# Two zeroed key buffers, a third engine for the key spreads of layer 0, and a new order, in a two-layer attention and token-mixing kernel

## The chip, the cores and the metric

The kernel runs on one core of a Trainium2 chip. The metric is the time of one execution on the device in microseconds (us), less is better. The engines of the core have short names here, those of the profile: PE is TensorE (matmuls; PEld its weight loads), DVE is VectorE, ACT is ScalarE, POOL is GpSimd, and SP is SyncE, which in this kernel issues all DMA transfers. Each engine works through a queue of its own in order; an instruction that must wait for another engine or a transfer waits on a semaphore at the head of its queue, and everything behind it waits too.

## The reference

`x` has 2048 tokens of 512 features, in bf16. Two equal layers follow one another; each is a part A and a part B, with one set of weights for both layers:

```python
x = x + A(layernorm(x), wqkv, wo)        # H = 32 heads of Dh = 16, window W = 256
x = x + B(layernorm(x), w1, b1, w2, b2)  # F = 1792
# A: scores = q k / 4 ; kept where 0 <= query - key < 256 ; softmax ; times v ; times wo
# B: u = gelu(h^T w1 + b1), which mixes tokens: (512 x 2048) (2048 x 1792); y = u w2 + b2, transposed back
```

## The kernel before

**Recorded operations and a written order.** The function does not issue instructions as it runs. Each step is recorded with `op(engine:kind, function, reads, writes, cost, ..., alts)` (`Graph.op`, L108): what it reads and writes, an estimated cost in ns, and in `alts` other engines that may do the same. `ORDER` (L15 to L43) is a compressed text, made beforehand by a planner that works with these costs; for each operation in turn it holds the operation's number and which of its alternatives is taken. `replay` (L176) decodes it, puts every operation at the end of the queue of its engine, and takes buffers from the pools (`Pool`, L56) as it goes; a buffer that is taken again makes its new writer wait for its old readers. `emit` (L197) then writes the queues, with one semaphore for each engine and 24 for transfers in turn. So a new ORDER can change the place of any instruction, the engine of those that have alternatives, and which buffers meet.

**Tiles.** Tokens go in four groups of 512, m = 0 to 3. `qkv(m)` (L528) makes queries, keys and values of a group: normalised tokens are transposed (`transpose`, L532: on PE for m = 0, by a DMA transpose of SP, L535, for the others), then multiplied by wqkv (`proj`, L553, for q and k, each in four parts o = 0 to 3 of 8 heads; `vproj`, L610, for v). All matmuls of projections, of wo, of u's parts and of y go through one helper line, L506. Results leave PSUM by a copy on DVE or ACT: queries `evq` (L564), values `evv` (L620, L622) into `vst`, from where SP spreads them to `vb` with four transfers (`vz`, L625).

**Keys.** Scores use the keys as weights in a block-diagonal form, `kbd[P, 3, 4, 8, 2, 64]` (L344): three buffers (the pool `p_kv`), one for each group in use. For each block of 64 keys two copies stand side by side, h = 0 and h = 1; in copy h only the partitions of the head with that parity hold keys, and the other 16 of each 32 partitions hold zeros. Group 0 writes both copies from PSUM, multiplied by the 0/1 columns `par` (`evka`, L574 on ACT or L575 on DVE). For the groups after it a copy `evk` (L586 on DVE, L588 on ACT) takes the keys to a staging buffer `stg`, and the key spread `kz` takes them from there to `kbd`, in one of two ways: `f_kz` (L590) is eight transfers of 16 KB on SP (L595), which write only the partitions that hold keys and so need zeros in the others already; `f_kz2` (L598) is two multiplications by `par` on POOL or DVE (L600), which write the zeros too. One line sets who may do it:

```python
if not layer and m < 3:
    ways = ways[:0:-1]
```

In layer 0, groups 1 and 2 write key buffers 1 and 2 for the first time and may use POOL or DVE only; group 3 takes buffer 0 again, whose zeros group 0 has written, and may use SP; so may all groups of layer 1.

**Attention.** `attention` (L653) goes over chunks of queries (`CHUNKS`, L331). A score `sc` (L679) multiplies keys and queries into two pairs of PSUM banks; two `exp` (L694, ACT) take them to bf16 probabilities `pt` (7 buffers), 128 x 1024 at a time as a rule; `mask` (L715, POOL) multiplies the edge blocks of the window by 0/1 words `ldm`; `pv` (L732) multiplies by the values, whose 17th column is ones (the memset `one`, L454) and gives the softmax's sums. DVE transposes the result (`od`, L752) and takes reciprocals (`rec`, L756); `prod` (L758, POOL or DVE) multiplies; `od2` (L763) transposes back. I count scores from 0 in the order of PE; layer 0 has 76 of them.

**The rest of a layer.** `wo_block` (L768) multiplies by wo (`fwo`) and adds to x (`res`, L774); a layer norm follows: statistics on DVE (`stat` L464, `agg` L466), `rstd` (L477) on POOL, normalising `xh` (L484) on DVE. u is summed over token groups as they come: `u_part` (L827) for the first tokens, with sums kept in `uT` (`evu`), and `u_last` (L846) for the last ones (`ful`, L853; `addu`, L864; gelu on ACT, L868). y (`y_block`, L886, kind `fy`, and `y_last` for the last tokens) multiplies by w2 and adds to x (`resy`, L894). w1 and w2 come from HBM in pieces of 128 KB on SP (`load_w1`, L783, L788; `load_w2`, L798, L800); each new piece waits until a buffer is free.

**Start.** Before the first layer, POOL writes the identity (`ident`: a memset L380, two selects L381 and L383) and the triangle for the masks (`tri`, L440 and L441); DVE makes `par`, `half` and `ldm` from them (L433 to L449) and warms PE with 42 matmuls. The first tokens' statistics, rstd and xh lead to the first keys (L574, L575), the first score and the first exponential, which starts at 9.23 us.

Of the kernel before, what the change touches and what calls it, by code (L numbers as in the profile page):

```python
# [14 lines left out]
ORDER = (  # L15
    'c-qZYJ&5Dl6~40X%xYimfEE<c1_ks$3o7(L4;)aTLJJCLK>;l&phATU2NZCjfD0ukpa&{ks1U)03KvsM;lhOjQ@C*9VgfE)xNzaZg$ox`xNyLQ3l}-^-'
    ';DQ%9mqm*W-MJ@-Jf&5^PTUig=m&x8#EXp8bY!nO0MoWh9R2vM_t$7>+eNTltlTbIJQ3qL12EE&*!#1FRrHR{$V`+Fha<*Oj8l@rpfWY<@rHtgZr|~gK'
    '>GZ*|u*d({`H+-*Ru$I5mFHahx4wJ(M<^t+x1172kzX9J-<IS(;`TvM8#W`cBnkFhyRoV8VDjhMOcwGf6@i{tULAvv-6L*7t>4BNl`W%dRJnj#HaVxcO'
    'qaSa6l)qabixrBc~$CzHu^!aeM8wOVCpLhES0nCW_#*=7vWZfDv2$Jsnhr|ERcfK@6w%wQOa836zT_zipG$yi!RnIcu~kI94m_aQR`pSV89{oIJ^e&GA'
    '9y6=af|HhRACumQ@C=84oTo2hWtT&rXYlr9FZ03VS^*BkAKShxjhGDfDR9Ti`s<mp>gS}kabzF|KRvO3Y`V7r>`qrzC$2!Lhw>uapn~Y}Yx>!KPFu$}~'  # L20
    'ih@)%QS0^k!Z!gXr2ucGz_|I`^Nf4L=yna$ghYuVw|!Ho@RdAgnT+Q}G0RvsV{^iCc}_Dev}<i!0PLpL?am3gdov!>H1i0y-E9lkG0yYcvMl#;y<YEj?'
    'i-q3JO9#kSl*0Q>rHfjAN9KT_q|@XJABh0K6E;rp5r+A?H$hD{1yzTrE^>>*Evmt6_YTDqO6r=lC;ZO{AMGh6(Cy>hCw4-HX7hf&=`#*iHP-Tt(Gae7b'
    '{v|GO8d5^73(6Q5Fk%AG1uzVAxkxRqA#n3AW-mo<OLn>$<f#iQ@zsp6e>LS}hC}1t65GqTp3Ml_jbw+cx5)$E^;WtEif$DfF1_GfYoW6uQ$9@7jhba$1'
    '_Ex(y58G+L<9P#`114?H0}u#JaFg2?f_B1tkkkffW8-5ZTDAxR>N49kdUyWNrv#C5}RP=c^J+<^id*OwP^zYk9woA*+TX}aBR!$1c1Oec%QqNrAS{F=V'
    'MzrXDbI0*6XmIlf~uUzksN5Zs6=)^Qa8j=e<)+?-1p;ek5jXG5*bQ&?~U?5-`vl+%I%9F%mQ5Yf&WUAvjt7?veWL48;SrA3X^=L&FAiV+-bPe&UAh{Sa'
    '<@<5J-_K)#t=u&|K@?OpKmj2_jRZl(^ZnE_UBW6vCa3`kVIWt6WS9mZC@+^Z;yCjIXn_DKk>?#r$}*16vg|GNX(Jrp@q8e^<>;*C;*{rQ`KKfaQKME13'
    'O=}m7@%32r2(mR=vWsF?RL8Wf5EU@AY8iv<^@63Qz}sQD1z`Uj4co*Q^l&tfmaAog2!_RAxvb9u_7x=(81Y!Ay22v<phRIr_(*=v?K$eP`j<^T9(POVH'
    'iB&I3|Lc5C7Ij>-E3euzQyM!}tG8M3_*mDHX*LWN{fqI{jC}SglqIK~U|PstT<BzDI+mth(K-^BP)t9=FEyfa)aR2ObOtAPDvV=t>5Cqcc$|but>YwFi'
    'd51S5uLwBCK;RxfHs5fo4qwOUO!1-Do>=?#*E9S)l*G>xoF)tb#Z10`02@};ri`o7h0dCx0Zjli^v(glPhPBbyERcnk5Wb^>s-&ufaWoZg{7R=`s6b;m'
    '^U-wmARQmnxbgHWVRDrz;EU+~;n@qRtUkr#=({&IdMK`QCj&*(GC%%u6rfs)z{IK4vHy{tH`m^#ESe8vSI4|C_%21K|EfDx_(z9(FMlehSDeZJ+pob(5'  # L30
    '2Dea(495WP3W%^y>-u&FoLQ|ph2465({)=spTYFFnM%I_wF9drwK#_StX0;FBFC|JmSHt43&FYd-as~R#dR#mqVHG^a$On~XIjOyfLA^btcNpEqiJjnh'
    'r<oW0f$XPmZ3n@G>$Q78OESuD3TR8Yiv@TP60lQ#u^$q#*W+&b=6Z5Jtt6oV6Pu0!-R}LA^U?qg~9>qclsURDh(($@9rA6KqI=<3TWCp$knxD+kiTRoI'
    '94KJFcKZ)OtnJK%{`8Bn*EPLImUu0}}9p0M3G}xP`3|64$XhSJnAyJ_F{d>SQvT&wwY!aA?eCvwJ8`rgN*1cAgUiP^T&QpCV+WgwZq=v|g?L(IMFL;bg'
    'LG3(#HJhN2iIl4VW?gcleKzrGcC1~JS{H%UR*NCUnMs3Z(0+l>#nAXG(gK{UcG0~LzK@N~Z~Os5EAlq{2oF$&x@%l15!c6;}}?}0MpQ55^w4}u12AlIo'
    'v+8oma4x0!Bnide|p`llJ1@WoId0t)Q6gb~xUaIf{ASx+hu7Q^|fyavNSQ5?C^v1@RiFm>;@k*8(8?@nl9syS4>9n>0V(Tk7N<h+q?_-QdkHhU^Ydk#c'
    '*1);JVE4EfKTLFeF@5NbdX^;`Vqt6eRszk<Q?@TjE%j)lPNNCRJVpXSwtJ6IS40^?%~st}YatErTC{?IN05J@9#oTzQ1KPQpzmlD7~IJ9@%j1%Q;xs$;'
    'A6*rA&SDsRVk``ez|{DKKB0#mCLAn=tD*OXyvD7G4|D~!yYG(O68-!2$xEwFZgxryT1N3hW*6S6-+92C>8&uuLXBi{2!LT+GBII-xQVb6@`v2mrkg?46'
    '7$U%3mJz>Wn@0S$3YXv~L$%A4eT}UZ3%$j=L2P08ojdAk5N}pNGDS#Y=~orP9k{!Iw^*^7^dzo1m0W>G-Zz`W&$%`cI&o-t6HyhW}|2De4)t=Yh}gr_S'
    'hqHs_ES>S^b1GK50^H+F-_7jjiDQuUc2T(YIKuf^g=4ll^nzEL`5=IUh{bmaHtojT<XeL}8t^9Ot!0f*ox&X+%xlrlQ@oijrnUVn*@ugg!|IyLE|e4Hs'
    ')Djk*R>HZw1LuU!<`}p<=v#X~$Ux1_d?%aoiUlm11;mb0FM|=&}=LFivUyQ?-7?fdX`Rch0AJHp+y9~=uk)9wsMf<GuN|$9=I=?<$&w(Br2h>XE1LNBS'  # L40
    'DW3(dD9IA_wNngH)bkp?)PWa^$==E9Gf>n8;V48s*W-)DsV6t6Gpi3$K%vW76m>!RGs{oPL;aUB_(GX^!8X+YM!imaeRiyzpnoRj=o#LhE6T;duloFHB'
    'EMr`{{hz3RoV'
)  # L43
# [262 lines left out]
def bass_interleave_layers__sliding_block__mixer_token_mlp__prompt_kernel(  # L306
# [28 lines left out]
    with es:  # L335
# [117 lines left out]

        f_one = lambda e: e.memset(vst[:, :, :, :, 16:17], 1.0)  # L454
# [73 lines left out]
        def qkv(m, before, split, layer):  # L528
            tx, tq, tk = Tile(p_xhT), Tile(p_qT), Tile(p_kv)
# [23 lines left out]
            def proj(o, which, a, b, wide):  # L553

                n, key = b - a, (filler(m == 0), which)
                ft = key[0]
# [12 lines left out]
                if m == 0:  # L569
# [18 lines left out]
                   alts=[("scalar", lambda e: e.copy(stg[:, ts.slot, 0:n], at()), act_cost(n))])  # L588

                def f_kz(e):  # L590
                    got = []
                    for h in range(2):
                        for r in range(4):
                            p = 32 * r + 16 * h
                            got.append(e.dma_start(kbd[p:p + 16, tk.slot, o, a // 64:b // 64, h, :],  # L595
                                                   stg[p:p + 16, ts.slot, 0:n].rearrange("p (s n) -> p s n", n=64)))
                    return got
# [376 lines left out]
```

## Time and profile before

| | |
|---|---|
| runs before, us | 443.46, 442.91, 442.94 (median 442.94) |
| the profiled execution's own time, us | 441.94 |
| its span in the profile, us | 440.2 |
| granted TensorE clock | 1.000 |
| key spreads (kz) in layer 0: POOL, DVE, SP | 6, 3, 3 |
| key spreads in layer 1: POOL, DVE, SP | 3, 5, 4 |
| last exponential of layer 0 ends, us | 154.05 |
| last matmul ends, us | 436.6 |

The profile is of one execution. A row of a group gives the line, the engine and the operation, the tiles (written <- read) with their shapes, the count, then after a bar the busy time in us and the mean ns of one, and after another bar the idle time of the engine just ahead of them with what ended it. A row of a timeline gives the start and the length in us of a run of like instructions, with the idle time before it in brackets. Where several instructions of one engine overlap in its pipeline, the durations add up to more than the time that passes. The row of busy tenths cuts the span into 40 equal slices of 11.0 us.

### The profile page before, as it was taken

What the parts mean: (1) busy time and instruction counts of PE and PEld (TensorE: products, weight loads), DVE (VectorE), ACT (ScalarE), POOL (GpSimd) and SP (SyncE); (2) the same over time, 40 slices, a digit from 0 to 9 for tenths busy, and PEclk for the clock granted to TensorE, in tenths of its full rate; (3) what the DMA queues carried; (4) which work ended last, traced back from release to release, by engine and by line L of the source; (5) the groups of instructions that cost most, each with busy time, mean ns of one, the idle gap of its engine ahead of it and who ended that gap; (6) DMA issues with size and microseconds to landing.
All of it is one profiled execution on the core that took longest, in us unless ns stands there. A gap on an engine that the chain in (4) does not pass through costs nothing.

```text
span 440.2 us, 13923 instructions
## 1 busy us (share of the span) xinstructions
PE 422.9 (96%) x5992; PEld 187.6 (43%) x5992; DVE 311.1 (71%) x570; ACT 318.5 (72%) x364; POOL 225.4 (51%) x344
## 2 busy tenths in 40 slices
PE   7998998999999999999999999999999999999996
PEld 6543333344333444444444444443443444434452
DVE  6999888887887678475768868899987746512223
ACT  5999999999999913618999999999999950420000
POOL 2687898778677610011574877877666631000000
PEclk9999999999999999999999999999999999999999
DMA  7752423203225365533351651140223346773513
GB/s 243 206 96 64 112 51 66 60 13 72 44 43 147 106 177 158 145 99 78 92 112 37 140 118 25 47 102 17 51 60 86 90 132 179 205 200 112 157 53 101
DMA packets 99885, 45.09 MB, mean 102 GB/s; under 512 B 30064, under 2 KB 99824, under 8 KB 99824
## 3 DMA queue, kind: packets, MB, share of 16 engines
q1 hardware_dynamic: 99824, 44.21, 39.2%
q8 instruction: 47, 0.77, 0.7%
q14 instruction: 14, 0.11, 0.1%
HBM read 33.56 MB, written 2.10 MB: 81 GB/s over the span
## 4 chain that ended last, share of the span: by engine, by line
PE 71%; ACT 19%; DVE 3%; POOL 3%; DMA 2%; issue 1%; SPq 0%; DVEq 0%
PE PS L506 49%; ACT pt L694 19%; PE PS L853 8%; PE PS L679 7%; PE PS L732 7%; POOL pt L715 3%; DMA w2b<-in_B_w_dram 2%; DVE stats L464 1%; DVE rl L752 1%; DMA x_sb<-in_A_x_dram 0%; DVE xh_sb L484 0%; DVE x_sb L774 0%; PE PS L542 0%; DVE vst L620 0%; DVE x_sb L894 0%
## 5 line engine op out<-in xcount | busy, mean ns | idle before, releaser
L694 ACT ACTIVATE pt<-PS 128x1024 bf16<-128x1024 f32 (+1 forms) x304 | 281.5, 1042 | 11.8 <-PE PS L679 9.6
L715 POOL TENSOR_TENSOR pt<-pt,ldm 128x256 int32<-128x256 int32 (+1 forms) x270 | 177.2, 682 | 78.9 <-ACT pt L694 78.4
L506 PE MATMUL PS<-uT,w2b 128*128 128x512 bf16 (+1 forms) x294 | 69.7, 370 | 1.1 <-DMA w2b<-in_B_w_dram 0.9
L506 PE MATMUL PS<-xhT,wqkv 128*128 128x512 bf16 (+1 forms) x288 | 67.1, 358 | 2.7 <-ACT pt L694 0.8
L506 PE MATMUL PS<-xh_sb,w1b 128*128 128x512 bf16 x280 | 69.0, 381 | 0.4 <-ACT pt L694 0.3
L679 PE MATMUL PS<-qT,kbd 32*128 32x256 bf16 (+4 forms) x1488 | 60.7, 252 | 5.5 <-ACT pt L694 3.7
L477 POOL TENSOR_TENSOR rstd<-agg,mhalf 128x2 f32<-128x2 f32 (+1 forms) x33 | 23.2, 703 | 58.8 <-DVE agg L466 55.9
L894 DVE SCALAR_TENSOR_TENSOR x_sb<-PS,b2col,x_sb 128x512 bf16<-128x512 f32 x31 | 22.9, 744 | 40.8 <-PE PS L506 40.6
L679 PEld LDWEIGHTS PS<-qT,kbd 32*128 32x128 bf16 x1488 | 21.7, 93 | 65.1 <-ACT pt L694 44.8
L752 DVE STREAM_TRANSPOSE rl<-PS 128x1024 f32<-128x1024 f32 x32 | 39.7, 1240 | 13.3 <-PE PS L732 12.8
L868 ACT ACTIVATE uT<-rl,b1col 128x512 bf16<-128x512 f32 x28 | 18.7, 714 | 39.9 <-DVE rl L864 39.9
L732 PE MATMUL PS<-pt,vb 64*17 64x320 bf16 (+4 forms) x2976 | 43.0, 252 | 2.1 <-DVE x_sb L774 0.6
L464 DVE BATCH_NORM_STATS2 stats<-x_sb 128x6 f32<-128x512 bf16 x64 | 43.0, 680 | 2.2 <-DMA x_sb<-in_A_x_dram 1.5
L506 PEld LDWEIGHTS PS<-uT,w2b 128*128 128x128 bf16 x294 | 26.7, 98 | 33.6 <-issue 3.1
L506 PE MATMUL PS<-uT,pt 128*128 128x512 bf16 x168 | 40.9, 380 | 0.0
L732 PEld LDWEIGHTS PS<-pt,vb 64*17 64x17 bf16 x2976 | 31.3, 85 | 17.2 <-POOL pt L715 5.6
L506 PEld LDWEIGHTS PS<-xh_sb,w1b 128*128 128x128 bf16 x280 | 23.9, 98 | 32.1 <-issue 5.7
L853 PE MATMUL PS<-xh_sb,w1b 128*128 128x512 bf16 x168 | 37.0, 380 | 0.0
L506 PEld LDWEIGHTS PS<-xhT,wqkv 128*128 128x128 bf16 x288 | 23.9, 97 | 30.2 <-issue 6.0
L484 DVE TENSOR_SCALAR xh_sb<-x_sb,agg,rstd 128x512 bf16<-128x512 bf16 x64 | 30.6, 498 | 7.6 <-POOL rstd L477 7.6
L506 PE MATMUL PS<-wqkv,xhT 128*128 128x512 bf16 x128 | 34.4, 381 | 0.2 <-ACT pt L694 0.2
L506 PE MATMUL PS<-wo_sb,oT 128*128 128x512 bf16 x128 | 32.5, 381 | 0.3 <-DVE oT L763 0.2
(58 smaller groups left out, 313.1 us busy)
## 6 DMA issues: line engine op xcount, KB each, us to landing
w1b<-in_B_w_dram SPq DMA_DIRECT2D x112, 128.0 KB, 2.7
w2b<-in_B_w_dram SPq DMA_DIRECT2D x70, 128.0 KB, 2.6
pt<-in_B_w_dram SPq DMA_DIRECT2D x42, 128.0 KB, 3.0
vb<-vst SPq DMA_DIRECT2D x64, 68.0 KB, 2.1
out_dram<-x_sb SPq DMA_DIRECT2D x15, 128.0 KB, 1.8
x_sb<-in_A_x_dram SPq DMA_DIRECT2D x3, 512.0 KB, 8.1
wqkv<-in_A_wqkv_dram SPq DMA_DIRECT2D x4, 256.0 KB, 4.2
kbd<-stg SPq DMA_DIRECT2D x56, 16.0 KB, 2.0
```

The lines of the kernel that those rows point to most:

```text
L464: op("vector:stat", lambda e: e.bn_stats(st[:, 0:6], x_sb[:, t, :]), reads=[f"x{t}"], writes=[("st", i)], cost=dve_cost(512))
L477: op("gpsimd:rstd", lambda e: e.tensor_tensor(rstd[:, t0:t1, 0], agg[:, t0:t1, 1], mhalf[:, 0:1].to_broadcast([P, t1 - t0]), op=ALU.pow), ...
L484: op("vector:xh", lambda e: e.tensor_scalar(xh_sb[:, t, :], x_sb[:, t, :], agg[:, t, 0:1], rstd[:, t, :], op0=ALU.subtract, op1=ALU.mult), ...
L506: return e.matmul(o, lhsT=w, rhs=x, start=start, stop=stop, skip_group_check=True)
L679: last = e.matmul(bank(tt[r // 2], r % 2)[:, base + c0 * 64:base + (c0 + n) * 64], lhsT=kbd[32 * r:32 * r + 32, tk.slot, o, jj].rearrange( ...
L694: op("scalar:exp", lambda e, ts=ts, tp=tp, i=i, cols=cols: e.activation(probs(tp)[:, i, 0:cols, :], pair(ts)[:, :, 0:cols].rearrange("p r ...
L715: return e.tensor_tensor(v, v, m, op=ALU.mult)
L732: last = e.matmul(bank(t, h)[32 * r:32 * r + 17, i + q0 * 64:i + (q0 + n) * 64], lhsT=vb[64 * h:64 * h + 64, tk.slot, jj, 4 * o + r, :], r ...
L752: op("vector:od", lambda e, t=tod, tr=tr: e.transpose(rl[:, tr.slot:tr.slot + 2].rearrange("p a b -> p (a b)"), pair(t)), reads=[(tod, i) ...
L853: last = e.matmul(bank(tu, tt), lhsT=v()[:, sc - b0, k0 + tt * P:k0 + (tt + 1) * P], rhs=xh_sb[:, sc, :], start=(sc == b0), stop=(sc == NT ...
L868: op("scalar:gelu", lambda e, ft=ft, tt=tt: e.activation(uT[:, ft, :], rl[:, tmps[tt].slot], ACTF.Gelu_apprx_tanh, bias=b1col[:, ft:ft + 1 ...
L894: op("vector:resy", lambda e: e.scalar_tensor_tensor(x_sb[:, t, :], bank(ft), b2col[:, t:t + 1], x_sb[:, t, :], op0=ALU.add, op1=ALU.add), ...
```

## The change

Two operations are added: POOL fills key buffers 1 and 2 with zeros, each as 2048 float32 words a partition (4096 bf16). Every key spread reads their result. In layer 0 SP becomes the last alternative for the key spreads of all groups, and an assertion holds that it is not used for buffer 0 by groups 1 and 2. ORDER is new as a whole, made with the two zeros and the new alternative.

```diff
--- before.py
+++ after.py
@@ -13,33 +13,32 @@
 
 
 ORDER = (
...
 )
 
 def begin_order(n):
@@ -453,6 +452,9 @@
 
         f_one = lambda e: e.memset(vst[:, :, :, :, 16:17], 1.0)
         op("gpsimd:one", f_one, reads=["mhalf"], writes=["one"], cost=200, alts=[("vector", f_one, 200)])
+        for k in (1, 2):
+            op("gpsimd:zero", lambda e, k=k: e.memset(kbd[:, k].rearrange("p a b c d -> p (a b c d)").bitcast(dt.float32), 0.0),
+               writes=["kz0"], cost=1900)
 
 
         op("vector", lambda e: e.memset(stats[:, :, :, 6:9], 0.0), writes=["eps0"])
@@ -589,6 +591,7 @@
 
                 def f_kz(e):
                     got = []
+                    assert layer or m > 2 or tk.slot
                     for h in range(2):
                         for r in range(4):
                             p = 32 * r + 16 * h
@@ -601,9 +604,9 @@
                                                0.0, op0=ALU.mult, op1=ALU.add)
                     return last
                 ways = [("sync", f_kz, 700), ("gpsimd", f_kz2, 1340), ("vector", f_kz2, 2 * dve_cost(n, 0.25, ptrs=1), True)]
-                if not layer and m < 3:
-                    ways = ways[:0:-1]
-                op(ways[0][0] + ":kz", ways[0][1], reads=[ts] + [("par", h) for h in range(2)],
+                if not layer:
+                    ways = ways[:0:-1] + ways[:1]
+                op(ways[0][0] + ":kz", ways[0][1], reads=[ts, "kz0"] + [("par", h) for h in range(2)],
                    writes=[(tk, "k", o, h, k) for h in range(2) for k in KEYS(a, b)], cost=ways[0][2], lock=len(ways[0]) > 3,
                    issue=5600.0, dma=ways[0][0] == "sync", parts=8, prio=-2e5, alts=ways[1:])
 
```

What the new order does, in counts and places. PE has the same 5992 matmuls. Key spreads in layer 0: POOL 5, DVE 2, SP 5 (both of group 1 for o = 2 and 3, one of group 2, two of group 3); in layer 1: POOL 5, DVE 4, SP 3. Products (`prod`): POOL 17, DVE 15 (12 and 20 before). Key copies (`evk`) on ACT 3 (4 before), first-group key multiplies (`evka`) on ACT 3 (4 before), query copies (`evq`) on ACT 8 (6 before), copies of u's parts (`evu`) on ACT 4 (3 before). The memset `one` goes from POOL to DVE.

On POOL the first zero stands behind the two selects of the identity and ahead of the first two rstd; the triangle's memset and select stand behind these. The second zero stands behind the mask of score 6. On SP, the spread of group 1's o = 2 follows two value spreads, and the spread of o = 3 follows six loads (w1, w2). On PE the order of scores is the same; the work ahead of each score in layer 0 differs by at most 1.7 us. The value matmuls of scores 16 to 20 come in two halves, which both stand between scores 23 and 24 before; in the new order the first half stands ahead of score 23 and the second between scores 23 and 24, and score 23 gets other PSUM banks. At the end, three groups of y's matmuls stand ahead of the last matmuls of `u_last`.

More of the change, by code (lines that the diff above doesn't have):

```diff
@@ L15 @@
 ORDER = (
[L16 to L39, printed above, removed]
@@ L40 @@
-    ')Djk*R>HZw1LuU!<`}p<=v#X~$Ux1_d?%aoiUlm11;mb0FM|=&}=LFivUyQ?-7?fdX`Rch0AJHp+y9~=uk)9wsMf<GuN|$9=I=?<$&w(Br2h>XE1LNBS'
-    'DW3(dD9IA_wNngH)bkp?)PWa^$==E9Gf>n8;V48s*W-)DsV6t6Gpi3$K%vW76m>!RGs{oPL;aUB_(GX^!8X+YM!imaeRiyzpnoRj=o#LhE6T;duloFHB'
-    'EMr`{{hz3RoV'
+    'c-pmAJ&5br6~40X?7Q#nO}GI)P@x3{?t&H+(1HS5&;t=vsL+BI^uUD+2VA&tp@0`uxKQE31QjkE@Pdm8DB!|{3l}aNaN)v*3l}b?aN)v*3l}B~!Nmk}W'
+    'Y2i)_hy&u%kCMCbfx=yzVn^$SnedODN2knQDjVp+hTzTLQLETf#aB><9Od%mi3M?<Bv@LI(W~R#HwZM-OBrR37wYfj;FKfJL}zKI<ekLOg9W^&=<wGB3'
@@ new lines @@
+    'R=#6~%)nwmRL-rY(OlolcVRY&xHdZ<Ch!jrmPC41BQ~iekCUzpNF4g3m0|v?rw^Hu#saOt_|LTvIvUP)eo!WHN!LEXxSPpQ@^amdmVOVhwR$y+16!*wJ'
+    '}uJ`XnAcxyYhedpBcb)=ii^?EHy(u6P2LQxL<FyK2r9HeQ#M|Znj4FF*LcZyP3EEn?yg-M}4&bAs1M&r>~QP^NeBq?~`Znr6IJ8`eqlbO`$-gen$6Pnc'
+    '|5%qY^8qHE>f38O5N_nxUR;$xc3aj-}R9?U)rA=|Sds7Vuwc1GKy;@kU(sEj<_`c_r$}q9+!6}16P|`F>EqIFW*wRLl?;!-{d~T-oH^gy9qmgK5ws!2l'
+    'F*b(dDVnZDk*4XoLSa)?(*gi4g9nDuVzH;2w`4pXTXwf=iK1@6rMFrwLI6VuyGXk<j$@J}2qj4ZXwYh9u-R-_zdxnqw|Kp}%WSjV-fcI5?fbhutQ^Oyc'
+    'zu7r_V)jBoVEA*-i_yz@hFb*axpOHi$UKs$78eG?GA<m*EM$zi_;!suIu)aq}go3UiG?EF2`}BRyUHwI2>BWzR@6XFs)vX%b8WHl_kcd5-yiVBUCCu_}'
@@ new lines @@
+    'w7z;i1W@YOFVFa8*-*xnPn61k{y*qI@Mu;{)9(NlV7fX1ha36i1HZ)M|b$3@a^Y`Z26li!v-dS!QqnyPcz{B104dGF)BFxDLh@rG-*LahggPuoJVqsn>'
+    'G~R{(Ne84W8C2u_GhB+(Wn(-b9HlDMS!@I7lv<Tb+>bCn+s=x``xR93u5RxI1L3Iyn`X^<N`NJSVfGcoO_SsHaZ9kh86(EZw{gb1h}^(Xy4LVY#jLsLM'
+    'VPNm)Mv}xu)WG_Z`Ba|dcb>>S5DJbjEXl5mv>I$b)wU-Tzuo5&-093_Oby6(3Zd*ery-jFrnz3m+u8SGwT=i5}byQ79Xyv$jWJ{`U@UbK@8TVvmIJE0b'
+    'Y}LdCQ$#0<Sgn@IAy}bMu;LN~IErXZR1m=IsweZl&62lIdcARPG*UR6ir?P0l;1;CzkmykoC?^eQrS_|YPYmnO^g0e`#x^Okny$zYyjP;h7%YMevtvBP'
+    'mz$pU{I|(z^a5yJis)H5~c52#YPwwi<L^D0K<ZyAZ6%K0%5Ui_=k)T33*KjB!!OAe!FjiDrovfTjP~s8mrX;lxs`@S<oEROK)#GwEdu%5aLFo0cs>!mL'
@@ new lines @@
+    'v@+>1&<N59kM#X!>8ZY(I?s@^{~9dW`W+?R!N5W!di5+v$|y#bPwsZnw5Qv?2fQR<QbfHlIu*ux<q5fqX?Sr2!p|+@WPNHk-{fL<P%&gDW6~-4>+?Qsp'
+    '(``+GnJ7H=!cLYe0p4VJVL)@SwJc-(BVM%e3BR5eK62Wspa<tQy?0jkG!4<pw{UX}s~o2KV@t|N*L^C*BKdAjMCmY&Jy+A^(~X&7HQt^*Q!a6Namx{H_'
+    'THvNb6cRu2rgGw2ex#D+sHC;C?$cn12iPS72I2kCErU4_g_ZoP;4Z~r!r~=vm$;0{lPxIMK*C(8}Rkbi24M!2E#Ar0cu<GDzV>U|*0gU5QKtYmao7e<*'
+    'JMH%Uy}fVkK#%*t=>QJh?znDJPhfT&!>cNa6)`9W1tX|bE8c3g^SmXH#4$ipTnkb!C?tv6<PSbBaM!h6jQ<S}&x1nbh>)+EWm}lIvl()yQ&-yU2(i}4g'
+    'hGWf4Fc7LsH<&Fqlk0g4}6@-kTtPnG=%c^aKJb87DLEZtJboGF_gjC4A#YHI2n&akj6n84u`{8x0^svT;xF23TqHRjEk75QKYIv-z%3rRw`p`V_%YLzU'
@@ new lines @@
+    '70EnPxq+EHzy<3<(kqN>#@G^B^k^4-bq|Xc)%Cw)gj0gjYyZJEa-$49eVm{LgWgi-TiE-a;)S{XXaEmrc}YpjMpt6+-H9^p~g}Mc646#)SevSSm7zNul'
+    '8TmUYLllIfk6m1u4wdDao%3RS2g1`;BUkbof3#7t~3N)cfU=!*2N-Qs-F<Hpoz)qufS_a@$SJN4xfE!y)%8P$N_jgS(I;zkonQ|Le|Mgg1va>_??P$&j'
+    'L2})5w0ZG^Mku6(_>xsB1mzr`z)%7-VbhRu=CO05g6{U}L9ceIG)D$RjzVF*M=TzD4#0R#S6AEcb(Po2}u(>)|t-!l+s^G!4w@l@O+>ujxBTvZPT?c*)'
+    '+;(7C8cLBiE)582rKm<h40gbYHB_|0pf1a48b^B%icGZ`6w77ecZ;K9r5F}V6&(4#*hD}xw+8-O85M)THZ@Qc%>b$8Sv5OC_km?_y?S+Oze1mAf*^d-t'
+    'n7BY;C6!^TUa<5Liy}d{=EL<*VDZG({;2{6XQJC@#Cv}{(7?<{AJhKKKrO~)x4aV%e{E?oAZ%B_9?pwr#JX<iBG2|xtwt96!68Ar#AQvo#&pXg@rd)8='
@@ L43 @@
+    'Tzw(7PW2_uLYWkEbx50e;-)3Ej+7Fai7(KJ*Om%blK&Yvu&uV_aS^e8CanrStuNBzhrQDEDLN<WBt`4F75Pa_EV3&+wi7xjM6Oo+h9RfS*U5L4929X`v'
+    'qr;WZJ?Uj_7w0QGb2H!psrKRZ5;EPElhZfMqVlgoYnLTqwZxa3Y8MOWg0o&xi^@cHBStC0N!`5>X*;QUcWP6CoYzT_`Q<R9N(LsR(aAmm?kJCDwe=RT5'
+    '{GZN&9sOVzs#eiJyH2dbli;L4_PUBP3VSL4#&xGUegqKKl9E(r6ik}_MU(!%Gf6c$_<po;#mmoO1{js1vX)}K8IzF!bzJx^hSxEpy$X$}*?2m9Ql2=mr'
+    'p$va&J-lG0@Vwx&JY37fvnoFqypw*P&viNRvFl1nejyqCU;P&@A}f3<UcbgcKMe1)YX34@{o0QH7qHM$z5'
 )
```

## The prediction

> **What bounds the kernel now.** Line numbers are those of the kernel before. I read first how busy each engine is, then the busy tenths in 40 slices, then the chain of work that ended last. From the page:
>
> ```profile
> PE 422.9 (96%) x5992; PEld 187.6 (43%) x5992; DVE 311.1 (71%) x570; ACT 318.5 (72%) x364; POOL 225.4 (51%) x344
> ...
> ACT  5999999999999913618999999999999950420000
> POOL 2687898778677610011574877877666631000000
> ...
> PE 71%; ACT 19%; DVE 3%; POOL 3%; DMA 2%; issue 1%; SPq 0%; DVEq 0%
> ```
>
> The matmuls fill 96% of the span on average, but the ACT row shows nines in slices 2 to 14, that is from 11 to 154 us, layer 0's attention: there the exponentials are back to back and TensorE has gaps. From about 154 us on TensorE is the bound: it is busy 10.00 of 10 us in each stretch from 160 to 290 us in the busy time by stretches, and after 356 us only transfers of w2 stop it. The chain agrees: ACT holds 19%, all of it in layer 0, and PE 71%. An edit in layer 0's attention is worth what it does to the exponentials; one in layer 1 what it does to TensorE.
>
> The timeline of ACT from 40 to 66 us, around the first key spreads (start, us, ..., idle before and releaser):
>
> ```profile
> 42.64 7.44 ACT L694 ACTIVATE pt<-PS 128x1024 bf16<-128x1024 f32 x8 [0.38 <-PE PS L679]
> 49.88 0.67 ACT L588 CAST stg<-PS 128x512 bf16<-128x512 f32 x1
> 50.35 2.05 ACT L694 ACTIVATE pt<-PS 128x1024 bf16<-128x1024 f32 x2
> 53.44 13.10 ACT L694 ACTIVATE pt<-PS 128x1024 bf16<-128x1024 f32 x14 [1.04 <-PE PS L732]
> ```
>
> ACT loses 1.04 us at 53.44, ahead of score 23's exponential, whose probability buffer the value matmuls (L732, right behind that score on TensorE) have to free; 0.38 at score 18; and 0.47 (50.35 less 49.88) to a copy of keys.
>
> **The two zeros.** Neither is in the trace, so I bound them by POOL's memsets:
>
> ```profile
> L380 POOL MEMSET ident<- 128x128 bf16 x1 | 0.2, 204 | 0.3 <-POOLq L959 0.3
> L454 POOL MEMSET vst<- 128x128 bf16 x1 | 0.7, 650 | 0.0
> L385 POOL MEMSET mhalf<- 128x1 f32 x1 | 0.1, 98 | 0.0
> ```
>
> 128 elements a partition take 204 ns, one takes 98: (204 - 98) / 127 = 0.83 ns an element. A zero is 2048 float32: 98 + 2047 x 0.83 = **1.8 us**. If time goes by bytes, float32 elements cost twice a bf16 one: 3.5 us. L454, 4.3 ns an element, writes one element in each 17 and is no model for a contiguous write (it would give 8.9 us). I take 1.8, the rows nearest in shape, and keep 3.5 as the upper end.
>
> The first zero stands on POOL behind the two selects that make the identity and ahead of the first two rstd. In POOL's timeline:
>
> ```profile
> 1.56 0.29 POOL L383 TENSOR_SCALAR_AFFINE_SELECT ident<-ident 128x128 bf16<-128x128 bf16 x1
> 1.81 0.29 POOL L441 TENSOR_SCALAR_AFFINE_SELECT tri<-tri 128x128 bf16<-128x128 bf16 x1
> 3.98 0.56 POOL L477 TENSOR_TENSOR rstd<-agg,mhalf 128x1 f32<-128x1 f32 x1 [1.88 <-DVE agg L466]
> ```
>
> POOL is free from 1.85 (select's end) to 3.98, that is 2.13 us; the triangle's two operations move behind the rstds, where only the masks wait for them, from 12 us on. At 1.8 us the zero ends at 3.65 and costs 0; the cover is DVE's statistics. At 3.5 it ends at 5.35, 1.4 us late, and rstd, xh, the first keys and the first exponential are one chain: +1.4 whole. The second stands behind score 6's mask at about 23 us, where POOL waits 1.11 us for the exponential of score 7; masks have several scores of slack, so 0 (at 3.5 us too). The Trainium skill (GPSIMD Engine Reference, "3.1 Elementwise — side-by-side cycle accounting") puts a tight loop on this engine at 1.8 cycles an element, 512 in 769 ns; by that a zero would take an estimated 3.1 us and the start would be about 1 us late. The rows above, at 0.83 ns, speak against it.
>
> **DVE from 10 to 40 us.** The busy time by stretches gives DVE 9.89, 9.77 and 9.53 of 10 us there, so what it is given extra is late. The new order gives it one key multiply pair that ACT had (L575, 0.87 us for two in its timeline), and puts a statistic (0.68 us) ahead of copies that a score waits for: **+1.55 us** by scores 13 to 17. The memset of ones that moves to it is a row of 0.17 us and fits in the 0.81 us that is left idle. Bounds: 0 (all of it in gaps) and +2.2 (with a second statistic). ACT works less by 0.2 to 0.9 us before these scores, which gains nothing while DVE is late.
>
> **Scores 18 to 23.** This lag eats stalls of before: score 18's 0.38 goes (the score is late anyway), and so does the key copy on ACT, 0.47. Of the 1.04, half goes: the first value block now stands ahead of score 23 and frees the buffer in time, but it has taken the PSUM banks that this score had, which now waits for the second exponential of score 22. From that exponential's end a score takes 0.40 us and its exponential starts 0.06 later, so some 0.5 stays: -0.5. The bounds: at score 72, where value matmuls stand ahead of a score that waits in the same way, ACT lost 0.90, which leaves -0.14; -1.04 if the matmuls are early. Late next are the masks of these value matmuls. Net with the lag: 1.55 - 0.38 - 0.47 - 0.5 = **+0.2 us** (from -1.9 to +1.2).
>
> **The key spreads moved to SP.** In layer 0, SP takes five instead of three, POOL five instead of six, DVE two instead of three; DVE and POOL win 0.7 to 1.45 us each, beside ACT's bound: 0. But each spread on SP is eight transfers, and SP issues in order:
>
> ```profile
> 92.24 6.15 SPq L595 DMA_DIRECT2D kbd<-stg  x8
> ...
> 106.04 5.64 SPq L595 DMA_DIRECT2D kbd<-stg  x8
> ```
> ```profile
> kbd<-stg SPq DMA_DIRECT2D x56, 16.0 KB, 2.0
> ```
>
> The first new one follows two value spreads (vb, which end at 49.8 in SP's timeline): 49.8 + 6.15 + 2.0 landing = 58.0. Score 26, its user, starts at 58.38 before. The second: transposes end near 59.3; + 5.8 + 2.0 = 67.1, used by score 31 at 67.5. Margins of 0.4 us each: I take **0**. Behind them on SP wait w1 transfers and transposes of the third group, needed after 70 us: 0. Bounds: -0.5 (POOL, 9.6 of 10 busy from 50 to 70 us, gives masks earlier) and +1.6 a spread, from the slowest landing of this tile (3.6 us against 2.0).
>
> **The rest.** Layer 0 after score 31 has the same order on TensorE to within 1.7 us of work: 0. Layer 1 gives POOL two spreads (1.45 each) and two products (L758, 1.06 against 0.79 on DVE) more; TensorE bounds and a score of slack hides each: 0 to +0.5, taken as 0. The tail:
>
> ```profile
> 388.81 1.47 PE L506 MATMUL PS<-uT,w2b 128*128 128x512 bf16 x6 [0.52 <-DMA w2b<-in_B_w_dram]
> ...
> 395.35 1.90 PE L506 MATMUL PS<-uT,w2b 128*128 128x512 bf16 x8 [0.42 <-DMA w2b<-in_B_w_dram]
> ```
>
> TensorE loses 0.94 us to w2. The new order mixes the first output matmuls, whose w2 came early, with the last matmuls of u, so the late w2 blocks are met later: -0.6 (from -0.94 to +0.9, the same wait twice).
>
> **Sum.** 0 (zeros) + 0.2 (start to score 23) + 0 (spreads) + 0 (the rest) - 0.6 (tail) = -0.4 us. The profiled execution took 441.94 us (span 440.2, 1.7 around it): 441.5. The median of the runs shown is 442.94, 1.00 above: **442.5**. A measurement of this kernel tells about 0.2%, 0.9 us, from no change; the forecast lies inside.
>
> **Rivals.**
> 1. *Forecast*, 442.5, own range 441.6 to 443.3: 0.42, of it 0.15 below 442.05.
> 2. *A key spread on SP lands late* (other side). Place: scores 26 and 31; it decides from 0.4 us of delay on. If one lands like the slowest, 3.6 us, ACT stands 1.2 us; with SP held by a transfer ahead of it as long again, 2.0: 443.7 to 444.5; both: up to 446.5. For it: a margin of 0.4, and eight transfers in line. Against it: the median of 56 landings is 2.0. 0.17, all slower.
> 3. *The lag is not recovered*: DVE stays full and the stalls of scores 18 and 23 only move: +1.55 instead of +0.2, 443.9. For it: DVE is 9.12 of 10 busy from 50 to 60 us too. Against it: 7.84 from 60 to 70. 0.13: 0.03 within, 0.10 slower.
> 4. *A zero is long or stands in DVE's way*: 1.4 us at the start, 443.9. The listing of the normalising line shows how far POOL can hold DVE (ns, least, median, most):
>
> ```profile
> L484 DVE TENSOR_SCALAR xh_sb<-x_sb,agg,rstd x64: 314/407/1118, 4.7 to 369.8; 128x512 bf16<-128x512 bf16 x64
> ```
>
>    314 ns at 79.38 with POOL idle, 1118 at 283.30 where POOL's product had begun at 283.21. An xh that starts within the second zero would wait up to 1.8 - 0.4 = 1.4 us, on a DVE that is full: the same 443.9. The Trainium skill (SBUF — State Buffer, "Who interferes with whom") has the rule: a DVE operation in a two-port mode and a POOL operation exclude each other for a whole instruction. By that rule the trace agrees (0.31 to 1.12 us). Against the case: near 23 us DVE mostly reads PSUM. 0.08, slower.
> 5. *More gain*: the lag stays in DVE's gaps and the tail wins all: -1.38 - 0.94 = -2.3, 440.6, or half of it, 441.7. 0.17, faster.
> 6. *The change does not do what it says*: one POOL spread and one DVE spread fewer free nothing that bounds, and the rest is a reshuffle that evens out: 442.9. 0.03, within.
>
> Faster 0.15 + 0.17 = 0.32; within 0.27 + 0.03 + 0.03 = 0.33; slower 0.17 + 0.10 + 0.08 = 0.35. The range, 440.4 to 444.8, takes in case 5 and case 2 with one late spread.
>
> **What would show it.** Two POOL memsets of 1.8 us, the first ended before 3.98; the first exponential near 9.23. The exponential of score 17 late by 1.0 to 1.6, that of score 24 within 0.3 of 55.27. An idle of ACT of some 0.5 before score 23, none over 0.3 before 26 and 31. The last exponential of layer 0 ends near 154.2 instead of 154.05. TensorE's idle for w2 near 0.3. The forecast is wrong if the first exponential is late, if ACT idles on kbd transfers, or if layer 1 has gaps that it had not.

## The result and the profile after

The changed kernel took **441.01 us** (median of 5 runs, 440.41 to 441.39) against 442.94 (5 runs, 441.96 to 443.53): a ratio of 0.9957, 95% interval 0.9941 to 0.9972, or 1.9 us less. Measured once more later, beside other runs of the kernel before, it gave 0.9955 (0.9941 to 0.9968). That is faster by more than the 0.2% that I had set as the bound; I had forecast 442.5, inside that bound, with 0.32 for faster. The time lies in the whole range, but below the forecast's own range of 441.6 to 443.3, and three quarters of the gain were not in my sum.

The profiled executions differ by less than the medians: 441.33 us after (span 439.6) against 441.94 (span 440.2). The reason is that the shown profile of before is one of its faster executions; a second profile of it took 443.92 us. One pair of profiles is not enough for an effect of this size, and most of what follows rests on seeing the same place in many.

The page after, the lines that answer to those shown of before:

```profile
PE 423.1 (96%) x5992; PEld 187.3 (43%) x5992; DVE 306.8 (70%) x562; ACT 317.8 (72%) x364; POOL 234.2 (53%) x352
...
ACT  5999999999899921628799899999999960530000
POOL 4799779878876521011576577879876541000000
...
PE 77%; ACT 18%; DVE 4%; issue 1%; POOL 0%
```

TensorE has the same work; POOL has 8.8 us more, the two zeros, products and layer 1's spreads; in the chain, DMA's 2% are gone, and those were mostly transfers of w2 at the end. POOL's timeline at the start and near 23 us:

```profile
1.66 1.80 POOL L456 MEMSET kbd<- 128x2048 f32 x1
4.00 0.56 POOL L479 TENSOR_TENSOR rstd<-agg,mhalf 128x1 f32<-128x1 f32 x1 [0.54 <-DVE agg L468]
...
22.91 1.80 POOL L456 MEMSET kbd<- 128x2048 f32 x1
```

Each zero takes 1.80 us. The first ends at 3.46, and rstd, at 4.00 (3.98 before), still waits 0.54 us for DVE's aggregate, not for the zero. ACT's timeline, the stretches that a wait opens:

```profile
22.43 29.88 ACT L697 ACTIVATE pt<-PS 128x1024 bf16<-128x1024 f32 x32 [0.49 <-PE PS L682]
52.91 9.27 ACT L697 ACTIVATE pt<-PS 128x1024 bf16<-128x1024 f32 x10 [0.60 <-PE PS L682]
62.92 10.19 ACT L697 ACTIVATE pt<-PS 128x1024 bf16<-128x1024 f32 x11 [0.74 <-PE PS L682]
```

At 22.43 (score 7) DVE's lag shows. In the chain ahead of it stands a normalising multiplication (xh) beside POOL's masks, more than twice as long as the like one in the kernel before (first line before, second after):

```profile
19.83 0.37 DVE L484 TENSOR_SCALAR xh_sb<-x_sb,agg,rstd 128x512 bf16<-128x512 bf16 x1
19.60 0.94 DVE L486 TENSOR_SCALAR xh_sb<-x_sb,agg,rstd 128x512 bf16<-128x512 bf16 x1
```

At 52.91 (score 23) 0.60 is left of the 1.04 us of before; the wait at 62.92 (score 28) was 0.05 before. TensorE's timeline shows no engine or transfer of the kernel that it waited for there, but a gap inside the score itself, five matmuls in; score 58 has another:

```profile
61.67 0.36 PE L682 MATMUL PS<-qT,kbd 32*128 32x128 bf16 x5
62.53 0.34 PE L682 MATMUL PS<-qT,kbd 32*128 32x320 bf16 x7 [0.50 <-issue]
...
120.05 0.39 PE L682 MATMUL PS<-qT,kbd 32*128 32x128 bf16 x9 [0.49 <-issue]
```

How the time of the two first profiles parts, from the starts of the exponentials and the end of the matmuls (us, after less before; all work on TensorE is the same, and where its order differs between two points the work is taken out):

| up to | after less before |
|---|---|
| first exponential | +0.01 |
| score 8 | +0.82 |
| score 17 | +0.85 |
| score 24 | -0.53 |
| score 30 (gap inside score 28) | +0.15 |
| score 75, end of layer 0's attention (gap inside score 58) | +0.76 |
| score 151, end of layer 1's attention | +1.16 |
| last matmul | -0.55 |

So the whole gain of this pair, 1.71 us, is made behind score 151. There TensorE's timeline of after has no wait. That of before has the two waits for w2 that were shown with the prediction; first the lines just ahead of them, then those of after:

```profile
386.41 1.89 PE L506 MATMUL PS<-uT,w2b 128*128 128x512 bf16 x8
...
391.41 3.51 PE L506 MATMUL PS<-uT,w2b 128*128 128x512 bf16 x14
```
```profile
385.34 0.59 PE L508 MATMUL PS<-uT,w2b 128*128 128x512 bf16 x2
385.77 1.03 PE L508 MATMUL PS<-uT,pt 128*128 128x512 bf16 x4
386.64 1.46 PE L856 MATMUL PS<-xh_sb,w1b 128*128 128x512 bf16 x6
387.93 0.59 PE L508 MATMUL PS<-uT,pt 128*128 128x512 bf16 x2
388.36 0.59 PE L856 MATMUL PS<-xh_sb,w1b 128*128 128x512 bf16 x2
388.80 1.89 PE L508 MATMUL PS<-uT,w2b 128*128 128x512 bf16 x8
```

The matmuls of y (L508) and the last ones of u (L856) take turns. In the kernel before the L853 lines end first, at 386.4, and y then runs into blocks of w2 that are not there. The new order also changes in what order SP loads w1 and w2 behind score 148; no run parts this from the order on TensorE.

The waits cost more than the 0.94 us of idle time printed before them. Matmuls of 512 columns that do not wait start 0.216 us apart, though each is recorded with 0.38 us; idle time is counted from the end of the one before, so each wait costs some 0.16 us more than is printed. In the kernel before, the eight matmuls from 386.41 on and the wait behind them fill 2.40 us up to 388.81, where eight without a wait take 1.73; the fourteen from 391.41 on fill 3.94 us up to 395.35, where 3.02 would do (in the trace two waits stand here, one of 0.15 us at 393.02, which the timeline does not print). From start to start TensorE loses 0.68 + 0.31 + 0.59 = 1.58 us to w2 in this profile, which is nearly the whole 1.71.

### The profile page after: what moved, and what is told of

Read it like the earlier page. It is cut to its first block, busy times and chain, and to the rows that moved or that the text cites. A ratio compares the mean times of both kernels' runs of the same rounds, so it can differ in the third digit from the quotient of the medians.

```text
span 439.6 us, 13924 instructions
## 1 busy us (share of the span) xinstructions
PE 423.1 (96%) x5992; PEld 187.3 (43%) x5992; DVE 306.8 (70%) x562; ACT 317.8 (72%) x364; POOL 234.2 (53%) x352
## 4 chain that ended last, share of the span: by engine, by line
PE 77%; ACT 18%; DVE 4%; issue 1%; POOL 0%
PE PS L508 53%; ACT pt L697 18%; PE PS L856 8%; PE PS L682 8%; PE PS L735 6%; PE PS L391 1%; DVE kbd L577 1%; DVE stats L466 1%; DVE xh_sb L486 0%; DVE rl L755 0%; DVE vst L623 0%; PE PS L544 0%; ACT xhT L553 0%; DVE x_sb L897 0%; DVE agg L468 0%
## 5 line engine op out<-in xcount | busy, mean ns | idle before, releaser
L718 POOL TENSOR_TENSOR pt<-pt,ldm 128x256 int32<-128x256 int32 (+2 forms) x270 | 177.2, 682 | 66.5 <-ACT pt L697 63.5
L508 PE MATMUL PS<-xh_sb,w1b 128*128 128x512 bf16 x280 | 69.5, 381 | 0.5 <-DVE xh_sb L486 0.3
L508 PE MATMUL PS<-xhT,wqkv 128*128 128x512 bf16 (+1 forms) x288 | 66.2, 357 | 2.5 <-ACT xhT L553 0.7
L508 PE MATMUL PS<-uT,w2b 128*128 128x512 bf16 (+1 forms) x294 | 68.2, 369 | 0.0
L508 PE MATMUL PS<-uT,pt 128*128 128x512 bf16 x168 | 41.4, 379 | 0.0
L508 PEld LDWEIGHTS PS<-uT,w2b 128*128 128x128 bf16 x294 | 27.2, 98 | 31.1 <-issue 3.5
L856 PE MATMUL PS<-xh_sb,w1b 128*128 128x512 bf16 x168 | 38.3, 379 | 0.0
L508 PEld LDWEIGHTS PS<-xh_sb,w1b 128*128 128x128 bf16 x280 | 23.5, 97 | 33.0 <-issue 6.6
L508 PEld LDWEIGHTS PS<-xhT,wqkv 128*128 128x128 bf16 x288 | 23.9, 97 | 30.5 <-issue 5.3
L508 PE MATMUL PS<-wqkv,xhT 128*128 128x512 bf16 x128 | 33.4, 381 | 0.3 <-DVE kbd L577 0.3
L508 PE MATMUL PS<-wo_sb,oT 128*128 128x512 bf16 x128 | 32.7, 381 | 0.0
L486 DVE TENSOR_SCALAR xh_sb<-x_sb,agg,rstd 128x512 bf16<-128x512 bf16 x64 | 28.9, 469 | 4.9 <-POOL rstd L479 4.7
```

Of the source, the lines that this page charges most:

```text
L486: op("vector:xh", lambda e: e.tensor_scalar(xh_sb[:, t, :], x_sb[:, t, :], agg[:, t, 0:1], rstd[:, t, :], op0=ALU.subtract, op1=ALU.mult), ...
L508: return e.matmul(o, lhsT=w, rhs=x, start=start, stop=stop, skip_group_check=True)
L718: return e.tensor_tensor(v, v, m, op=ALU.mult)
L856: last = e.matmul(bank(tu, tt), lhsT=v()[:, sc - b0, k0 + tt * P:k0 + (tt + 1) * P], rhs=xh_sb[:, sc, :], start=(sc == b0), stop=(sc == NT ...
```

## The experiments

Theory T at first: the tail makes the gain; zeros and new spreads make none. Rival Z: the zeros and the spreads on SP make it, in layer 0. An order is a list, so two can be joined: the first part of one, and then every operation that is left in the sequence of the other. Ratios are against runs of the kernel before on the same chip: it took 442.05 us beside the tail alone, the front alone, the whole zeros alone and the first run of the new order, 442.88 beside the zeros of one element, the second run of the new order and the kernels again, and 442.93 beside the last four. The times expected were worked out from 442.9.

**The tail alone.**

```diff
-ORDER of before, whole
+ORDER of before up to score 140, then the new ORDER's sequence
```

> The kernel before up to score 140 (layer 1), and from there on the operations in the order that the new ORDER has for them. No zeros, no new key spreads on SP. Theory T (the gain is made at the tail: the matmuls of y that stand ahead of the last matmuls of u let TensorE run through without the two waits for w2): TensorE idles for w2 0 instead of 0.94 us, time 441.3 to 441.9 (1.0 to 1.6 under the kernel before). Rival Z (the zeros and the key spreads on SP make the gain in layer 0, where score 24 came 0.5 earlier): 442.9, as before.

Measured: 442.47 us, ratio 1.0003 (0.9987 to 1.0019). The waits for w2 are 0, but the time is that of before. Its profile is 0.44 us behind the first profile of before at score 131, then 1.33 at score 141: at the seam a matmul of u waited 0.35 us, some 0.5 from start to start, for a residual addition of DVE, which neither whole order has. The tail then took 1.7 us less than in before. So the experiment is spoilt by its seam; it shows that the tail's saving comes with the tail's order, not what it is worth in all.

**The front alone.**

```diff
-the new ORDER, whole
+the new ORDER up to score 140, then before's sequence
```

> The changed kernel up to score 140 of layer 1, with zeros and key spreads on SP, and from there on the order of the kernel before. Theory T: the waits for w2 are back (0.9 us), time 442.6 to 443.2. Rival Z: the gain stays, 441.0 to 441.4.

Measured: 441.86 us, ratio 0.9995 (0.9982 to 1.0007). Against 442.05 the gain is gone, which speaks against Z, but the same seam costs 1.0 us here (from -0.18 at score 136 to +0.81 at score 146), and the waits for w2 are 0.4 instead of 0.9. It tells no more than the first.

**The zeros alone.**

```diff
 f_one = lambda e: e.memset(vst[:, :, :, :, 16:17], 1.0)
 op("gpsimd:one", f_one, ...)
+for k in (1, 2):
+    op("gpsimd:zero", lambda e, k=k: e.memset(kbd[:, k]...bitcast(dt.float32), 0.0), writes=["kz0"], cost=1900)
```

> The kernel before with nothing but the two zeros put in on POOL at the places that the change gives them (the triangle's memset and select moved behind the first two rstd as there); no spread uses them. Theory T: both zeros lie in POOL's gaps, first exponential at 9.2, time 442.9 within 0.3. Rival P (a zero holds DVE's operations or a mask): an xh or a value copy near 22 to 25 us is lengthened by up to 1.4 us, time 443.5 to 444.3.

Measured: 444.54 us, ratio **1.0053** (1.0034 to 1.0072), 2.4 us slower, and not for rival P's reason alone. In its profile no operation of DVE is lengthened near the zeros. POOL's timeline:

```profile
22.96 1.81 POOL L456 MEMSET kbd<- 128x2048 f32 x1
24.72 1.56 POOL L717 TENSOR_TENSOR pt<-pt,ldm 128x128 int32<-128x128 int32 x3
```

The next masks start at 24.72 instead of 23.66, 0.6 us late when the later start (0.47) is taken out; from score 8 to score 10 the exponentials fall 0.51 us further behind, of which other profiles of the old order have 0.1 to 0.4 without whole zeros. The larger part sits elsewhere: the warm-up matmuls at the start run slow to their end (first exponential +0.47), and a gap inside score 28, of the kind seen above, is 1.22 us long.

**The same with zeros of one element.**

```diff
-e.memset(kbd[:, k].rearrange("p a b c d -> p (a b c d)").bitcast(dt.float32), 0.0)
+e.memset(kbd[:, k, 0, 0, 0, 0:1], 0.0)
```

One element a partition is written, so the rest of the buffers is not zeroed; in this kernel, whose spreads write their own zeros there, nothing needs them.

> The kernel before with two memsets at the zeros' places that write one element a partition each (0.1 us instead of 1.8), the triangle's two operations moved as before. The run with whole zeros and nothing else was 2.4 us slower. If the time that the zeros take on POOL made that (theory P): this one is at 442.0 to 442.5. If the moved instructions and their code did (theory C: TensorE's stream of code arrives late at score 28, 1.2 us, and its clock rises late at the start, 0.5 us): 443.5 to 445 again, with the gap inside score 28.

Measured: 442.53 us, ratio 0.9989 (0.9975 to 1.0003): as before. So it is the duration of the zeros, not the two more instructions or the moved ones, that costs 2.4 us in the old order (theory P in the wider sense). How 1.8 us of POOL time turns into that stays open: the profile shows a few tenths directly, and the rest as a late clock and a gap inside score 28, which the profile with short zeros did not have. But a late clock is in six other profiles of both orders, and such a gap in the second profile of before, so that the zeros made either is not shown.

**The new order without zeros and without the three new spreads on SP.**

```diff
-for k in (1, 2): op("gpsimd:zero", ...)
-reads=[ts, "kz0"] + ...
+reads=[ts] + ...
 ORDER: spreads of group 1, o = 2 and 3, and group 2, o = 3
-    sync, sync, sync
+    gpsimd, vector, gpsimd (as before), at their places in the new order
```

> The new order without the two zeros, and with the three key spreads that only the zeros allow on SP put back on the engines of the kernel before (two on POOL, one on DVE), at their places in the new order. Theory T: 440.8 to 441.4, like the changed kernel. Rival Z: the POOL spreads delay masks from 50 to 70 us by 1.4 us each and the gain goes: 442.2 to 443.

Measured: 450.43 us, ratio 1.0190 (1.0168 to 1.0212). Neither theory had this. TensorE's waits, longest in total:

```profile
PE PS L677 <- POOL kbd L598: 4.4, 1, 4.4
...
PE PS L677 <- DVE kbd L598: 2.4, 1, 2.4
```

A place that does for SP, which starts the transfer as soon as it comes to it (48.86 us), is far too late in POOL's queue behind masks (61.06). The experiment tells of the place, not of the engine, so the next one gives the spreads places of their own.

```diff
 ORDER: the same three spreads on gpsimd, vector, gpsimd
-    at their places in the new order
+    behind the mask of score 22, the query copy and the mask of score 46, as in before
```

> The new order without zeros, the three key spreads back on POOL, DVE and POOL, and each at the place that it had in the kernel before (behind the mask of score 22, the query copy and the mask of score 46). Theory O (the new order makes the change's gain, the spreads on SP make none): 440.9 to 441.6, as the changed kernel. Theory S (POOL and DVE are so full from 50 to 70 us that the spreads must leave them): ACT waits for masks or keys at scores 24 to 31, 442.5 or more.

Measured: 443.56 us, ratio **1.0014** (1.0000 to 1.0027): theory S. The new order with its good tail, but without the zeros and the spreads on SP, gains nothing. ACT's timeline:

```profile
64.00 37.29 ACT L692 ACTIVATE pt<-PS 128x1024 bf16<-128x1024 f32 x40 [1.26 <-PE PS L677]
102.68 1.94 ACT L692 ACTIVATE pt<-PS 128x1024 bf16<-128x1024 f32 x2 [1.39 <-PE PS L677]
```

And what stands behind the two waits, from the chain of waits of this run between 58 and 66 us and between 94 and 103 us:

```profile
...
58.55 1.47 DVE kbd L598 x2
60.02 0.61 DVE stats L462
60.64 0.02 issue
60.66 0.33 DVE agg L464 x3
60.99 0.57 DVE vst L618
61.56 0.61 DVE stg L584
62.16 0.04 issue
62.21 1.40 PE PS L730 x93
...
```
```profile
...
95.68 3.88 POOL pt L713 x6
99.56 1.34 POOL kbd L598 x2
100.90 0.70 POOL pt L713
101.60 0.04 issue
101.65 0.64 PE PS L730 x37
...
```

The spread on DVE took 1.47 us in this chain, 1.55 in DVE's timeline (0.61 there at its place in before), and held up the copies that free TensorE's banks; the spread on POOL stood between masks, and value matmuls waited for the mask behind it. With the spreads on SP, neither wait is there. So taking them off DVE and POOL is worth 2.6 us to this order, even with the two zeros that it needs (1.0014 against 0.9955, measured beside the same runs of before, and 1.26 + 1.39 us in this profile). It is not worth that to the kernel before, where the same spreads at the same places cost ACT no such wait.

**The kernels themselves again.**

```diff
 (no edit: the changed kernel, and the kernel before)
```

> The changed kernel itself, once more, beside the same runs of the kernel before. If the first comparison measured the change: 0.994 to 0.997 of the kernel before. If the kernel before only happened to run at its upper end then (its runs spread over 3 us), 0.997 to 0.9995. Its second profile shows whether the two gaps of TensorE inside scores 28 and 58 (0.50 and 0.49 us, no releaser) come back at these places or are chance.

> The kernel before itself: a ratio of 1 within its interval, which gives the least difference that these runs can tell. Its second profile shows what of the first is chance: the two waits for w2 in the tail (0.52 and 0.42 us) and the number of slow warm-up matmuls at the start (31 of 42).

Measured: 441.03 us, ratio 0.9955 (0.9941 to 0.9968); and 443.38 us, ratio 1.0012 (0.9999 to 1.0024). The first comparison stands, and a kernel beside itself comes out 0.12% off, with an interval up to 0.24%. In the second profile of after the gap inside score 28 is gone and that inside score 58 is there again, 0.49 us. In the second profile of before the gap inside score 28 is there, 1.21 us, where the first had none:

```profile
62.28 0.36 PE L679 MATMUL PS<-qT,kbd 32*128 32x128 bf16 x6
63.85 0.34 PE L679 MATMUL PS<-qT,kbd 32*128 32x320 bf16 x6 [1.21 <-issue]
```

and its wait for w2, over 352 to 440 us, is longer than in the first (0.9):

```profile
PE PS L506 <- DMA w2b<-in_B_w_dram: 1.4, 2, 0.8
```

**The parts again, with seams where both orders have done nearly the same work.** Theory A: the parts add. Theory L: layer 0 makes the gain.

```diff
+layer0_only:      new ORDER to the end of layer 0's attention | before
+all_but_layer0:   before to the same place                    | new ORDER
+tail_from_148:    before up to score 147                      | new ORDER
+layer0_and_tail:  new ORDER to the end of layer 0 | before | new ORDER from score 148
```

> The changed kernel (zeros, key spreads on SP, new order) up to the end of layer 0's attention (the first wo matmuls behind score 75), the order of before from there on. The two cuts at score 140 each met a stall of their own (a u matmul that waited 0.5 us, and 1 us in all by score 146), so the parts are cut here at places where both orders have done nearly the same work. Theory A (the parts add: layer 0 -0.3 to -0.9, layer 1's attention +0.4, tail -1.5): ratio 0.998 to 0.9993. Theory L (layer 0 makes the whole gain): 0.995 to 0.9965.

Measured: 442.84 us, ratio 1.0003 (0.9989 to 1.0017): no gain, theory L falls. Part of it is a seam again: TensorE waits 0.4 us for w1 between 150 and 210 us, which the changed kernel does not, and 0.55 us are lost from score 75 to 76. Less that, layer 0 would be worth some -0.6 us; this is worked out, not measured, and its profile does not show it: at score 75 it stands 0.42 us behind the first profile of before, of which 0.47 is the late clock at the start.

> The kernel before up to the same place, without zeros and without the new spreads on SP, and the new order from there on. Theory A: -1.1 us, ratio 0.9970 to 0.9980. Theory L: 1.000 to 1.001.

Measured: 441.34 us, ratio 0.9969 (0.9955 to 0.9984), as theory A had it, or a little better.

> The kernel before up to the value matmuls behind score 147, the new order from there on. Theory A: TensorE does not wait for w2, 1.4 to 1.7 us less between score 151 and the end, ratio 0.9960 to 0.9972. Theory L: the time saved at the tail is only given back from waits that the same run had by chance: 0.999 to 1.001.

Measured: 441.45 us, ratio **0.9970** (0.9956 to 0.9983): 1.3 us from the tail alone, with a seam of 0.1 to 0.2 us in its profile.

> The changed kernel's layer 0 and its tail from score 148 on, with layer 1's attention in the order of before, which the profiles show 0.4 us shorter. Theory A: 440.4 to 440.9 where the changed kernel has 441.0, ratio 0.9940 to 0.9952, faster than both kernels. Theory L: 0.995 to 0.9965, the same as layer 0 alone.

Measured: 441.64 us, ratio 0.9976 (0.9962 to 0.9990). Slower than either expectation: layer 1 in the order of before gains nothing, and the seam behind layer 0 costs 0.8 us in its profile. No joined order beat the changed kernel.

The tail in all profiles. The wait of TensorE for w2 behind 352 us:

| tail in the order of | runs | idle before w2's matmuls, as printed, us | lost to w2 from start to start, us |
|---|---|---|---|
| before | before, before again, zeros, short zeros, front, layer 0 | 0.9, 1.4, 0.8, 0.6, 0.4, 1.5 | 1.58, 1.87, 1.19, 1.14, 0.69, 1.80 |
| after | after, after again, tail, order (two), all but layer 0, from 148, layer 0 and tail | 0 in all eight | 0 in all eight |

The mean of the upper row's last column is 1.4 us, close to the 1.3 that the tail gained. From score 151 to the last matmul, the eight of the lower row take 1.5 to 1.7 us less than the first profile of before; those of the upper row from 0.9 less to 0.5 more.

## Why the prediction was right or wrong

- **The zeros' price.** Right: 1.80 us each, against 1.8 worked out from 0.83 ns an element. The first fits in the 2.13 us and rstd is not late. The Trainium skill's 1.8 cycles an element (GPSIMD Engine Reference, "3.1 Elementwise — side-by-side cycle accounting"), which I had taken to an estimated 3.1 us, does not hold for a memset here.
- **That a zero on POOL at 23 us is free.** Right in this order, so far as its profile shows: behind the zero and one mask, POOL waits 0.89 us for an exponential. Put into the old order both zeros cost 2.4 us (1.0053), with one element 0 (0.9989). "Masks have several scores of slack" was read from the old POOL queue; the new order has another queue there.
- **DVE's lag of +1.55 us.** Right that DVE is late, twice too large (+0.8 by scores 8 to 17), and in part for another reason: at 18 us DVE's queue is 0.5 us late, and an xh at 19.6 that took 0.94 us beside POOL's masks instead of 0.37 adds 0.57, of which not all reaches the score. All seven profiles of the new order have this xh at 0.94. That POOL can hold an xh stood in the prediction, but for the zeros and not for the masks.
- **Scores 18 to 23.** Right step by step: score 18 gave 0.45 back (0.38 forecast), the key copy 0.46 (0.47), score 23's wait fell from 1.04 to 0.60 (0.5 left). With the smaller lag the net was -0.53 at score 24, not +0.2.
- **Scores 28 and 58.** Not foreseen: two gaps of 0.5 us inside scores, in which TensorE waits for its instructions, so far as the profiles can say (see the last section). At score 28 the gap comes and goes in both kernels (1.21 in the second profile of before, none in the second of after). At score 58 it is in all seven profiles with the new order there (0.17 to 0.49), and in two of the seven with the old one (0.15 and 0.16), so it is in the main a price of the new order; my 0 for layer 0 after score 31 was wrong by 0.6 us (from score 30 to 75, in both profiles of after).
- **The spreads on SP.** Right that they land in time: the first is issued from 48.86 to 55.02 us, 2.0 to land, and score 26 starts at 57.74. The 0 for moving them ("DVE and POOL win 0.7 to 1.45 us each, beside ACT's bound") may hold against the kernel before, where they cost ACT no wait of this size; it does not hold inside the new order: with the spreads put back, ACT waits 1.26 and 1.39 us. My rule that only ACT's time counts in layer 0 left out that DVE frees TensorE's banks, and POOL's masks release its value matmuls, in queue order.
- **The tail.** The mechanism was right and the size was off: -0.6 forecast; -1.3 measured with the tail alone. I added the two printed idle times to 0.94 us and took a part of that. From start to start the same profile loses 1.58 us to w2, and six profiles of the old tail lose 0.69 to 1.87; in the new tail it is 0, not a part. My lower bound of -0.94 was no bound.
- **Layer 1.** 0 to +0.5 forecast, taken as 0: the profiles show +0.4 to +0.5 from score 75 to 151 in both profiles of after, against -0.04 to +0.23 in the second of before and the two with zeros added.
- **Rivals.** None of the slower ones came: no late transfer of a spread, no zero at the start. The DVE lag was recovered by score 24. What came is the time of the fifth, "more gain", which had 0.17, but only half of its reason: the tail won all, and the lag did not stay in DVE's gaps.

In sum, from the medians: the tail -1.3 us, shown by the run from score 148, which has neither the zeros nor the new spreads. The rest is some -0.6 us, the difference to the whole, within the intervals of both, and where it comes from stays open. The profiles do not show it as a gain of layer 0: at score 75 five profiles of the new order with the spreads on SP stand 0.27 us ahead to 0.76 behind the first of before, and six of the old order without whole zeros 0 to 1.31 behind. So the two zeros and the third engine, without which this new order gains nothing, are not shown to gain by themselves. In the sum the mis-sized term is the tail; that the time still lies in the whole range is owed to that range's width.

## What to carry to other kernels

A wait is priced from start to start of the instructions around it and not by the idle time printed, since instructions overlap in the pipeline. And a wait for a transfer seen once in a profile has a spread of its own: look at several executions before a price is put on taking it away. An order that is written out is a whole: of joined parts, each seam cost 0.1 to 1 us, and three spreads on other engines at unchanged places cost 8 us, so the worth of one part is best asked by giving the moved work a place of its own. Work that is off the bounding engine is not free if its engine also empties the buffers of the bounding one in order.

## What the runs showed of the hardware

- TensorE's 42 warm-up matmuls start 107 ns apart at first, and from some moment on 56 ns apart. In 7 of the 14 profiles that moment came between 4.0 and 5.2 us from the span's start, and the warm-up ended at 5.0 to 5.6 us; in the other 7 all 42 were slow, the warm-up ended at 5.7 to 5.8 us, and the first exponential started 0.2 to 0.5 us later. The two profiles of the changed kernel differ in this (first exponential +0.01 and +0.47 against the first profile of before). The Trainium skill (TensorE: Matmul & The Clock Gate, "Part 1: The HAM clock gate (the "warmup" mystery)") gives the same two distances and a window that runs freely, so that the moment varies between runs; the trace agrees.
- TensorE's instructions come in pieces of 16 KB by a queue of their own (47 packets, 0.77 MB in each run, which is 64 bytes for each of its 11984 matmuls and weight loads). Around 60 us value matmuls and a score follow each other, more than 200 instructions in 2 us. In the three profiles with a gap inside score 28 the packet of the piece started 1.50, 0.86 and 0.86 us ahead of that score (after, before again, zeros), and the gaps are 0.50, 1.21 and 1.22 us; in the other eleven it started 2.07 us or more ahead, and there is no gap. At score 58 it started 1.74 to 2.21 us ahead in the nine profiles with a gap and 2.14 to 2.46 in the five without. In all twelve gaps TensorE went on 1.29 to 1.63 us after the packet had ended. So a late piece fits every gap; no run moved a piece to test it, and why a piece comes late is open.
- A DVE operation on SBUF beside POOL can be more than twice as long: the two multiplications of a key spread took 0.61 us at 58.2 in before and 1.55 at 58.5 in the new order with the spreads put back, where POOL's masks ran beside them; an xh took 0.37 us at 19.8 in before and 0.94 at 19.6 in after, again beside masks.
- Matmuls of 128x512 that do not wait start 0.216 us apart, and each is recorded with 0.38 us: in the kernel before, a wait printed as 0.52, 0.15 or 0.42 us made the next start 0.68, 0.31 or 0.59 us later than without it.
